# Moving one attention pair's loads ahead of the token weights, and the token weights' conversions behind an earlier pair's state chain

## The chip, the cores and the metric

The kernel runs on one core of one Trainium2 chip. The metric is the device time of one execution in microseconds; the kernel before took 613.91 us (median of three runs, 613.28 to 617.16).

## The reference, cut to what matters

A decayed linear attention in blocks feeds a token-and-channel mixer, and that feeds a Fourier mixer with a channel network.

```python
attn_out = _attn_ref(q, k, v, lam)             # B=2, H=8, S=768, D=64
x = attn_out.transpose(0, 2, 1, 3).reshape(B, S, H * D)
# _moe_ref
xt = x.transpose(0, 2, 1)
h = np.maximum(xt @ w_tok1, 0.0) @ w_tok2      # w_tok1 768x256, w_tok2 256x768
u = x + h.transpose(0, 2, 1)
x = u + np.maximum(u @ w_ch1, 0.0) @ w_ch2     # 512 -> 1536 -> 512
# _moe2_ref: 2-d FFT, norm, 512 -> 2048 -> 512
```

Inside the attention, each block has a scores part (`q k^T` times a decay mask, times `v`) and a state part (`q` times the running `k^T v` state, which decays from block to block).

## The kernel before, in words

The weights arrive as 64-bit words (the host passes double words of the numpy arrays) and are turned into float32 on the chip: ScalarE (ACT) makes `m_*` from the high words (L210), for channel weights also a shifted low word (L213); VectorE (DVE) merges the words (L235, L236, L238 for token weights, L233 and L238 for channel weights). ACT then rounds a high part `w_*` (L264) and GpSimd (POOL) subtracts it from the value for the low part (L265). One call of `convert` moves this chain on by one stage each. Three raw slots of 128x1024 words exist; a load into a slot waits until DVE's last merge has read the slot's old content.

The attention goes by pairs of heads, numbered 0 to 7: 0 to 3 are batch 0, 4 to 7 batch 1. The name of a tile holds the pair's number within its batch. For each pair `s` makes the scores on TensorE (PE) and masks them on DVE (L396), `u` scales `k` on ACT (L413), multiplies it with `v` on PE (L418) and runs the chain of states on DVE (L422 once, L424 four times), and `r` copies the states into a block-diagonal tile `att` on ACT (L435, first two blocks of states, then three), multiplies on PE (L441 with the masked scores, L444 with the states) and copies the result out to `xT` on ACT (L446). `l` loads a later pair: `kp`, then `q`, then `k` and `v` in one. `x` transposes half of a batch's result (PE L461) and splits it (ACT L117, DVE L118), `h` is the first token layer (PE L122 to L124, ACT L498, DVE L499), `o` the second, `m` a step of the channel network.

What stands where in this stretch is written out in the string `EARLY`. PE and SyncE (SP, which issues the loads) follow it literally. ACT, DVE and POOL have an order that a scheduler makes when the kernel is built; `tc.issue_after(ins)` keeps what is issued under it behind `ins`. Each engine runs its own list in order, so one instruction that waits holds all behind it.

The first token layer's three weight tiles are keyed `t1` (`raw_t_0d`, `raw_t_1d`, `raw_t_2d`, 512 KB each), the second's `t2` (`raw_t_0_0d` and so on, 384 KB each). The trace writes `raw_t_0d` for both kinds of the first one.

Of the kernel before, what the change touches and what calls it, by code (L numbers as in the profile page):

```python
# [15 lines left out]
AF = mybir.ActivationFunctionType  # L16
# [10 lines left out]
C = 128  # L27
# [6 lines left out]
BIG = 12 * NQ  # L34


EARLY = """s0 w u0 w s1 r0 u1 s2 u2 l4 r1 s3 c u3 r2 s4 l5 r3 u4 x00 s5 l6 u5 r4 s6 x01 h00 r5 c h01 l7 u6 s7 u7 r6 o00
r7 m o01 x10 m x11 m h10 m h11 m m o10 o11 k"""

WHEN = ((67, 71, 77, 73, 74, 77, 74, 77, 77, 79, 80, 81, 85, 83, 86, 85, 87, 84, 88, 90, 92, 91, 94, 97, 99),  # L40
# [21 lines left out]
def body(ctx: ExitStack, tc: tile.TileContext, qkv, kT, lam, w_tok1, w_tok2,  # L62
# [30 lines left out]


    on_act = {("table", 0): table_load}

    def acc_bank(n):
        return ps_acc.tile([P, 512], F32, tag="acc", name=n)
# [72 lines left out]
    def load_next():  # L171
        job = next_job()
        if job is None:
            return False
        kind, key = job
        at_["load"] += 1
        jobs.append(job)
        raw = raw_p.tile([P, 1024], U32, tag="raw", name="raw_" + "_".join(map(str, key)) + kind[0])
        raws[job] = raw
        if key[0] == "dft":  # L180
            nc.sync.dma_start(raw.bitcast(F32)[:, :512], dft[key[1]])
        elif kind == "sums":
            for i, k in enumerate(pair_keys(key)):
                nc.sync.dma_start(raw.bitcast(F32)[:, i * 512:(i + 1) * 512], singles[place_of(k)])
        elif kind == "single":
            nc.sync.dma_start(raw.bitcast(F32)[:, :512], singles[place_of(key)])
        else:
            w = {"t1": lambda: w_tok1[key[1]], "t2": lambda: w_tok2[key[1], key[2]],
                 "a": lambda: (w_ch1, m_ch1)[key[1]][key[2]], "b": lambda: (w_ch2, m_ch2)[key[1]][key[2]]}[key[0]]()
            nc.sync.dma_start(raw[:, :2 * width(key)], w)  # L190
        return True
# [5 lines left out]
    def stage_abs():  # L197

        if at_["abs"] >= at_["load"]:
            return  # L200
        job = jobs[at_["abs"]]
        kind, key = job
        at_["abs"] += 1
        if kind in ("single", "sums"):
            return
        m = raw_p.tile([P, 512], U32, tag="man", name="m_" + "_".join(map(str, key)), bufs=BUFS["man"])[:, :width(key)]
        mans[job] = m
        with tc.issue_after(on_act["out", 1]):
            lo, hi = words(job)
            nc.scalar.activation(f32(m), f32(hi), AF.Copy, scale=DOWN)  # L210
            if key[0] in "ab":
                halves = raws[job].bitcast(U16)[:, :4 * width(key)].rearrange("p (n t) -> p n t", t=4)
                nc.scalar.activation(lo, halves[:, :, 1], AF.Identity, scale=2.0 ** -13, bias=floor_by)  # L213
# [58 lines left out]
    def convert(n=1, among=()):  # L272

        among = list(among)
        for _ in range(n):
            if at_["part"] < at_["word"] and (jobs[at_["part"]][0] == "ahead" or room(jobs[at_["part"]][1])):
                stage_part()
            if at_["word"] < at_["abs"] and at_["word"] < at_["part"] + 1:
                for op in word_ops():
                    op()  # L280
                    if among:
                        among.pop(0)()
            while at_["load"] < at_["word"] + BUFS["raw"] and len(raws) < BUFS["raw"] and load_next():
                pass
            if at_["abs"] < at_["word"] + 1:
                stage_abs()
        for op in among:
            op()
# [116 lines left out]
    def attention_states(b, hp, dT, pw):  # L405

        n = f"{b}_{hp}"
        t, sts = pair[b, hp]
        kn, v = (t[:, i, :].rearrange("p (c j) -> p c j", j=C) for i in (1, 2))
        behind = (("table", 0), ("state", 0), ("out", 0), ("out", 1))[min(NP * b + hp, 3)]  # L410
        with tc.issue_after(on_act[behind]):
            for a in range(2):
                nc.scalar.activation(kn[:, :NC - 1, a * D:(a + 1) * D], kn[:, :NC - 1, a * D:(a + 1) * D], AF.Copy,  # L413
                                     scale=dT[:, 2 * hp + a, C - 1:C])
        ups = acc_bank(f"u_{n}")
        for c in range(NC - 1):
            for a in range(2):
                nc.tensor.matmul(ups[a * D:(a + 1) * D, c * D:(c + 1) * D], kn[:, c, a * D:(a + 1) * D],  # L418
                                 v[:, c, a * D:(a + 1) * D], start=True, stop=True)
        state = temp((NC - 1) * D, f"state_{n}").rearrange("p (c e) -> p c e", c=NC - 1)  # L420
        up = ups[:, :(NC - 1) * D].rearrange("p (c e) -> p c e", c=NC - 1)
        nc.vector.tensor_copy(state[:, 0], up[:, 0])  # L422
        for c in range(1, NC - 1):
            stt(out=state[:, c], in0=state[:, c - 1], scalar=pw[:, hp, C - 1:C], in1=up[:, c],  # L424
                op0=ALU.mult, op1=ALU.add)
        pair[b, hp] = t, sts, state

    def attention_out(b, hp, bd, bank):
# [560 lines left out]
    with tc.manual_schedule(engines={ENG.SP, ENG.PE}):  # L989
        dT, pw, kps, bds, skew = attention_setup()  # L990

        def load(n):
            load_kp(n // NP, n % NP, kps[n % NP])
            load_qkv(n // NP, n % NP)

        load(2)
        skew(6, H)
        load(3)
        for _ in range(3):
            load_next()  # L1000
        for b in range(B):
            xT[b] = big_tile(f"xT_{b}")[:, :4 * S].rearrange("p (k s) -> p k s", k=4)

        def scores(n):
            attention_scores(n // NP, n % NP, dT, pw, kps[n % NP])

        def states(n):
            attention_states(n // NP, n % NP, dT, pw)

        def result(n):  # L1010
            attention_out(n // NP, n % NP, bds[n % 2], x_bank if n == 7 else acc_bank)


        warm = acc_bank("warm")

        def keep_warm(n):
            for _ in range(n):
                nc.tensor.transpose(warm[:, :P], ident, ident)

        def constants():  # L1020
            rawx = temp(P, "rawx")
            nc.sync.dma_start(rawx, dft_x)
            nc.scalar.activation(cx, rawx, AF.Copy)

        keep_warm(22)
        acts = {"s": scores, "u": states, "r": result, "l": load, "c": convert, "x": token_in, "h": token_hidden,
                "o": token_out, "m": run, "w": lambda: keep_warm(8), "k": constants}
        for word in EARLY.split():
            acts[word[0]](*(int(i) for i in word[1:]))
        run(54 - step["i"])  # L1030
        free = big_tile("tops_0", F32R).rearrange("p (j k h s) -> p j k h s", j=2, k=2, h=2)
        half = half_tile([P, 2, 2, 2, HS], "tops_1", F32R)
        free = [free, big_tile("tops_2", F32R).rearrange("p (j k h s) -> p j k h s", j=2, k=2, h=2)]
        homes = {1: (free[0][:, 0], free[0][:, 1], half[:, 0]), 0: (free[1][:, 0], free[1][:, 1], half[:, 1])}
        pieces = [input_sums(0, k, homes[0]) for k in range(2)]
        for fn in pieces[0]:
            fn()
            run(1)
        run(62 - step["i"])
        for k in range(2):  # L1040
            for fn in input_sums(1, k, homes[1]):
                fn()
        run(64 - step["i"])
        input_sums_last(0, 0)
        for fn in pieces[1]:
            run(1)
            fn()
        run(len(todo) - step["i"])
        for k in range(2):
            input_sums_last(1, k)  # L1050
        pend = [(False, lambda: second(todo[-1]))]

        place = {"i": 0}

        def between():
            j, i = divmod(place["i"], 4)
            place["i"] += 1
            turns = TURNS_7[j] * (i + 1) // 4 - TURNS_7[j] * i // 4
            ends, fn = pend.pop(0) if pend else (False, lambda: None)
            if ends:  # L1060
                fn()
            convert(turns)
            if not ends:
                fn()

        for j, u in enumerate(by_seven):
            seven(u[0], u[1], between)
            last = j == len(by_seven) - 1
            todo_ = seconds(*u)
            if last:  # L1070
                for x in (todo_[0], todo_[2]):
                    second_of(*x)
                second_two(todo_[1], todo_[3])
            else:
                pend.extend([(x[4], lambda x=x: second_of(*x)) for x in todo_])
            if j == 0:
                input_sums_last(0, 1)
# [99 lines left out]
```

## Time and profile before

| what | value |
|---|---|
| median of three runs | 613.91 us (613.28 to 617.16) |
| the profiled execution | 616.56 us, of which the span of the trace is 614.5 us |
| mean granted TensorE clock | 0.997 |
| PE busy | 591.0 us, 96% of the span |
| DVE, ACT, POOL busy | 411.9, 269.8 and 142.6 us |
| moved by DMA | 65.58 MB, mean 107 GB/s |

The profiled execution lies 2.65 us above the median and 2.06 us of it lie outside the span. Times below are in microseconds from the span's start. A row of a timeline gives start, duration, engine, source line, operation, tiles and count, and in brackets how long the engine stood idle before it and what ended that.

### The profile page before, as it was taken

What the parts mean: (1) busy time and instruction counts of PE and PEld (TensorE: products, weight loads), DVE (VectorE), ACT (ScalarE), POOL (GpSimd) and SP (SyncE); (2) the same over time, 40 slices, a digit from 0 to 9 for tenths busy, and PEclk for the clock granted to TensorE, in tenths of its full rate; (3) what the DMA queues carried; (4) which work ended last, traced back from release to release, by engine and by line L of the source; (5) the groups of instructions that cost most, each with busy time, mean ns of one, the idle gap of its engine ahead of it and who ended that gap; (6) DMA issues with size and microseconds to landing.
All of it is one profiled execution on the core that took longest, in us unless ns stands there. A gap on an engine that the chain in (4) does not pass through costs nothing. (4 is left out here: it accounts for less than half of the span.)

```text
span 614.5 us, 9599 instructions
## 1 busy us (share of the span) xinstructions
PE 591.0 (96%) x3704; PEld 546.5 (89%) x3704; DVE 411.9 (67%) x768; ACT 269.8 (44%) x536; POOL 142.6 (23%) x119
## 2 busy tenths in 40 slices
PE   8789999999989999999999999999999999999997
PEld 7767799999989998999989899878888998998896
DVE  6697897792657337649696897789685477343435
ACT  2666984653546345244453462335553454211110
POOL 5254233220400220111263210024420232300000
PEclk9899999999999999999999999999999999999999
DMA  7965434333368247100132101002453132000005
GB/s 278 404 246 190 145 123 158 103 99 126 102 232 272 79 159 259 63 1 1 52 86 70 36 2 34 18 0 71 127 172 112 34 121 86 1 1 0 1 1 205
DMA packets 24637, 65.58 MB, mean 107 GB/s; under 512 B 2824, under 2 KB 3984, under 8 KB 24592
## 3 DMA queue, kind: packets, MB, share of 16 engines
q1 hardware_dynamic: 24304, 64.83, 31.5%
q8 instruction: 29, 0.48, 0.3%
q10 hardware_dynamic: 288, 0.14, 0.1%
q14 instruction: 16, 0.13, 0.1%
HBM read 54.99 MB, written 9.97 MB: 106 GB/s over the span
## 5 line engine op out<-in xcount | busy, mean ns | idle before, releaser
L124 PE MATMUL ac<-w_b,hid 128*128 128x512 f32 x192 | 75.9, 396 | 0.3 <-DVE hid L499 0.3
L123 PE MATMUL ac<-w_b,hid 128*128 128x512 f32 x192 | 75.7, 394 | 0.0
L122 PE MATMUL ac<-w_b,hid 128*128 128x512 f32 x192 | 74.9, 390 | 0.0
L499 DVE SCALAR_TENSOR_TENSOR hid<-ph,hid 128x384 fp32r<-128x384 f32 x68 | 37.7, 554 | 48.8 <-ACT hid L498 48.6
L123 PE MATMUL ac<-hid,w_b 128*128 128x384 f32 x192 | 65.0, 338 | 1.3 <-DVE hid L499 1.1
L122 PE MATMUL ac<-hid,w_b 128*128 128x384 f32 x192 | 65.2, 340 | 1.0 <-ACT hid L498 1.0
L122 PE MATMUL ph<-uh,w_a 128*128 128x384 f32 x192 | 64.7, 337 | 0.5 <-DVE hid L499 0.5
L498 ACT ACTIVATE hid<-ph 128x384 fp32r<-128x384 f32 x68 | 33.0, 485 | 71.7 <-PE ph L124 71.7
L124 PE MATMUL ph<-uh,w_a 128*128 128x384 f32 x192 | 64.3, 335 | 0.0
L124 PE MATMUL ac<-hid,w_b 128*128 128x384 f32 x192 | 64.2, 335 | 0.0
L123 PE MATMUL ph<-uh,w_a 128*128 128x384 f32 x192 | 64.2, 334 | 0.0
L265 POOL TENSOR_TENSOR w_a<-m_a,w_a 128x512 fp32r<-128x512 f32 x18 | 25.6, 1421 | 84.6 <-ACT w_a L264 66.5
L124 PEld LDWEIGHTS ac<-w_b,hid 128*128 128x128 f32 x192 | 36.0, 188 | 8.5 <-DVE hid L499 0.8
L123 PEld LDWEIGHTS ac<-w_b,hid 128*128 128x128 f32 x192 | 36.0, 188 | 6.1
L122 PEld LDWEIGHTS ac<-w_b,hid 128*128 128x128 f32 x192 | 36.1, 188 | 5.8
L265 POOL TENSOR_TENSOR w_b<-m_b,w_b 128x512 fp32r<-128x512 f32 x18 | 24.6, 1368 | 70.2 <-ACT w_b L264 45.6
L122 PEld LDWEIGHTS ac<-hid,w_b 128*128 128x128 f32 x192 | 36.1, 188 | 3.0 <-ACT hid L498 2.5
L123 PEld LDWEIGHTS ac<-hid,w_b 128*128 128x128 f32 x192 | 36.1, 188 | 2.9 <-DVE hid L499 2.9
L122 PEld LDWEIGHTS ph<-uh,w_a 128*128 128x128 f32 x192 | 36.1, 188 | 1.0 <-DVE hid L499 0.8
L123 PEld LDWEIGHTS ph<-uh,w_a 128*128 128x128 f32 x192 | 36.1, 188 | 0.1
L124 PEld LDWEIGHTS ac<-hid,w_b 128*128 128x128 f32 x192 | 36.0, 188 | 0.0
L124 PEld LDWEIGHTS ph<-uh,w_a 128*128 128x128 f32 x192 | 36.0, 188 | 0.0
(504 smaller groups left out, 1478.6 us busy)
## 6 DMA issues: line engine op xcount, KB each, us to landing
qkv<-qkv SPq DMA_DIRECT2D x7, 768.0 KB, 9.4
single_scratch<-m_a SPq DMA_DIRECT2D x16, 256.0 KB, 4.4
qkv<-qkv SPq DMA_DIRECT2D x10, 384.0 KB, 6.0
kp<-kT SPq DMA_DIRECT2D x8, 384.0 KB, 8.4
out<-u SPq DMA_DIRECT2D x11, 256.0 KB, 2.0
single_scratch<-m_b SPq DMA_DIRECT2D x10, 256.0 KB, 5.7
raw_t_0d<-w_tok SPq DMA_DIRECT2D x2, 384.0 KB, 9.1
raw_t_1d<-w_tok SPq DMA_DIRECT2D x2, 384.0 KB, 3.5
```

The costliest lines, as they stand in the source:

```text
L122: nc.tensor.matmul(ps, wt[0], xt[0], start=first, stop=False, **kw)
L123: nc.tensor.matmul(ps, wt[0], xt[1], start=False, stop=False, **kw)
L124: nc.tensor.matmul(ps, wt[1], xt[0], start=False, stop=last, **kw)
L265: nc.gpsimd.tensor_tensor(out=t[:, 1, :n], in0=src, in1=f32(t[:, 0, :n]), op=ALU.subtract)
L498: nc.scalar.activation(hi, ps, AF.Relu)
L499: stt(out=lo, in0=ps, scalar=0.0, in1=f32(hi), op0=ALU.max, op1=ALU.subtract)
```

## The change

`EARLY` is rewritten: the load of pair 4 (`l4`) stands first, then the three loads of the first token layer's weights as `n n n` (they stood ahead of `EARLY` before), the conversion calls `c` that bring those weights forward stand after `u3` and after `l5` and `l6`, and the third pair's result `r2` and the load of pair 6 lie between them. `mark` remembers the latest scaling of `k` on ACT and the latest step of the state chain on DVE, and `behind_urgent` keeps every conversion of a `t1` tile behind what was last marked.

```diff
-EARLY = """s0 w u0 w s1 r0 u1 s2 u2 l4 r1 s3 c u3 r2 s4 l5 r3 u4 x00 s5 l6 u5 r4 s6 x01 h00 r5 c h01 l7 u6 s7 u7 r6 o00
+EARLY = """s0 l4 n n n w u0 w s1 r0 u1 s2 u2 r1 s3 u3 l5 c c r2 l6 c c c s4 r3 u4 x00 s5 u5 r4 s6 x01 h00 r5 c h01 l7 u6 s7 u7 r6 o00
 r7 m o01 x10 m x11 m h10 m h11 m m o10 o11 k"""
+    urgent = {}
+    def mark(which, op):
+        urgent[which] = op.ins
+        return op
+    def behind_urgent(key):
+        stack = ExitStack()
+        if key[0] == "t1":
+            for ins in urgent.values():
+                stack.enter_context(tc.issue_after(ins))
+        return stack
...
-        with tc.issue_after(on_act["out", 1]):
+        with tc.issue_after(on_act["out", 1]), behind_urgent(key):
...
+                key = jobs[at_["word"]][1]
                 for op in word_ops():
-                    op()
+                    with behind_urgent(key):
+                        op()
...
-                nc.scalar.activation(kn[:, :NC - 1, a * D:(a + 1) * D], kn[:, :NC - 1, a * D:(a + 1) * D], AF.Copy,
-                                     scale=dT[:, 2 * hp + a, C - 1:C])
+                mark("act", nc.scalar.activation(
+                    kn[:, :NC - 1, a * D:(a + 1) * D], kn[:, :NC - 1, a * D:(a + 1) * D], AF.Copy,
+                    scale=dT[:, 2 * hp + a, C - 1:C]))
...
-            stt(out=state[:, c], in0=state[:, c - 1], scalar=pw[:, hp, C - 1:C], in1=up[:, c],
-                op0=ALU.mult, op1=ALU.add)
+            mark("dve", stt(out=state[:, c], in0=state[:, c - 1], scalar=pw[:, hp, C - 1:C], in1=up[:, c],
+                            op0=ALU.mult, op1=ALU.add))
...
-        for _ in range(3):
-            load_next()
```

PE's and POOL's lists are the same before and after, row for row. SP's list, from the fourth pair's `k` and `v` on, read before:

```order
L373 DMA qkv_3_170<-qkv 128x1536
L190 DMA raw_t_0d<-w_tok 128x1024
L190 DMA raw_t_1d<-w_tok 128x1024
L190 DMA raw_t_2d<-w_tok 128x1024
L377 DMA kp<-kT 128x768
L372 DMA qkv_0_380<-qkv 128x768
L373 DMA qkv_0_380<-qkv 128x1536
L377 DMA kp<-kT 128x768
L372 DMA qkv_1_513<-qkv 128x768
L373 DMA qkv_1_513<-qkv 128x1536
L377 DMA kp<-kT 128x768
```

and reads now:

```order
L390 DMA qkv_3_170<-qkv 128x1536
L394 DMA kp<-kT 128x768
L389 DMA qkv_0_223<-qkv 128x768
L390 DMA qkv_0_223<-qkv 128x1536
L205 DMA raw_t_0d<-w_tok 128x1024
L205 DMA raw_t_1d<-w_tok 128x1024
L205 DMA raw_t_2d<-w_tok 128x1024
L394 DMA kp<-kT 128x768
L389 DMA qkv_1_457<-qkv 128x768
L390 DMA qkv_1_457<-qkv 128x1536
L205 DMA raw_t_0_0d<-w_tok 128x768
L394 DMA kp<-kT 128x768
```

Pair 4's 1536 KB changed places with the three `t1` tiles' 1536 KB, and the first `t2` tile moved ahead of pair 6.

ACT's list around pair 3 (`qkv_3` and `state_3` are pair 3, `qkv_0` is pair 4, `qkv_1` pair 5, `po_2` and `po_3` the results of pairs 2 and 3) read before:

```order
L210 ACTIVATE m_t_0_437<-raw_t_0d 128x512
L413 ACTIVATE qkv_3_170<-qkv_3_170,att 128x5x64 x2
L210 ACTIVATE m_t_1_716<-raw_t_1d 128x512
L210 ACTIVATE m_t_2_726<-raw_t_2d 128x512
L413 ACTIVATE qkv_0_380<-qkv_0_380,att 128x5x64 x2
L446 ACTIVATE xT_179<-po_2_0_462 128x384
L264 ACTIVATE w_t_0_718<-m_t_0_437 128x512
L435 ACTIVATE att<-state_3_452 64x2x64 x2
L446 ACTIVATE xT_179<-po_2_1_474 128x384
L264 ACTIVATE w_t_1_734<-m_t_1_716 128x512
L435 ACTIVATE att<-state_3_452 64x3x64 x2
L413 ACTIVATE qkv_1_513<-qkv_1_513,att 128x5x64 x2
```

and reads now:

```order
L430 ACTIVATE qkv_3_170<-qkv_3_170,att 128x5x64 x2
L225 ACTIVATE m_t_0_460<-raw_t_0d 128x512
L225 ACTIVATE m_t_1_467<-raw_t_1d 128x512
L430 ACTIVATE qkv_0_223<-qkv_0_223,att 128x5x64 x2
L225 ACTIVATE m_t_2_511<-raw_t_2d 128x512
L453 ACTIVATE att<-state_3_450 64x2x64 x2
L464 ACTIVATE xT_173<-po_2_0_473 128x384
L453 ACTIVATE att<-state_3_450 64x3x64 x2
L464 ACTIVATE xT_173<-po_2_1_485 128x384
L279 ACTIVATE w_t_0_503<-m_t_0_460 128x512
L430 ACTIVATE qkv_1_457<-qkv_1_457,att 128x5x64
L279 ACTIVATE w_t_1_513<-m_t_1_467 128x512
```

Pair 3's scaling now stands ahead of `m_t_0`, and its state copies ahead of the rounding of the token weights, but behind all three `m_t` of the `t1` tiles.

Later on ACT, from the first token layer's second half (`h1s_1_0`) to pair 6's state copies (`state_2`), the list read before:

```order
L498 ACTIVATE h1s_1_0_829<-h_0_1_810 128x512
L413 ACTIVATE qkv_3_834<-qkv_3_834,att 128x5x64
L210 ACTIVATE m_b_0_1029<-raw_b_0d 128x512
L213 ACTIVATE raw_b_0d<-raw_b_0d,floor_by 128x512
L435 ACTIVATE att<-state_2_850 64x2x64 x2
L210 ACTIVATE m_a_1_1039<-raw_a_1d 128x512
L213 ACTIVATE raw_a_1d<-raw_a_1d,floor_by 128x512
L435 ACTIVATE att<-state_2_850 64x3x64 x2
```

and reads now:

```order
L516 ACTIVATE h1s_1_0_829<-h_0_1_810 128x512
L279 ACTIVATE w_a_1_1131<-m_a_1_1039 128x512
L225 ACTIVATE m_a_2_1138<-raw_a_2d 128x512
L228 ACTIVATE raw_a_2d<-raw_a_2d,floor_by 128x512
L453 ACTIVATE att<-state_2_850 64x2x64 x2
L279 ACTIVATE w_b_1_1156<-m_b_1_1064 128x512
L225 ACTIVATE m_b_2_1163<-raw_b_2d 128x512
L228 ACTIVATE raw_b_2d<-raw_b_2d,floor_by 128x512
L279 ACTIVATE w_a_2_1205<-m_a_2_1138 128x512
L453 ACTIVATE att<-state_2_850 64x3x64 x2
```

Four instructions instead of two stand between pair 6's two groups of state copies, and the channel weights converted there are of later tiles; pair 7's scaling (`qkv_3_834`) moved up ahead of these rows.

## Rows read from the trace of the kernel before

**Rows 1.** The page, part 1: busy time, share of the span, instructions.
```profile
PE 591.0 (96%) x3704; PEld 546.5 (89%) x3704; DVE 411.9 (67%) x768; ACT 269.8 (44%) x536; POOL 142.6 (23%) x119
```

**Rows 2.** Table by stage: stretch, length, busy by engine, clock, DMA share, GB/s.
```profile
25.00:60.00 35.00, 30.61 (x393) 26.15 (x390) 28.98 (x61) 24.47 (x54) 14.82 (x11) 1.00 0.64 241
60.00:75.00 15.00, 13.60 (x163) 11.68 (x161) 13.29 (x27) 12.25 (x26) 5.87 (x4) 1.00 0.54 187
75.00:110.00 35.00, 34.42 (x206) 32.01 (x203) 26.98 (x42) 21.89 (x42) 10.72 (x8) 1.00 0.38 123
30.00:35.00 5.00, 3.33 (x55) 2.82 (x50) 5.00 (x12) 2.22 (x6) 2.10 (x2) 1.00 1.04 411
```

**Rows 3.** Waits of PE, 25 to 75 us: total, times, longest.
```profile
PE po L444 <- ACT att L435: 2.8, 4, 1.7
PE u L418 <- ACT qkv L413: 1.4, 2, 0.9
```

**Rows 4.** Timeline of ACT around pair 3 and the first transposes.
```profile
26.39 0.66 ACT L210 ACTIVATE m_t<-raw_t_0d 128x512 f32<-128x512 f32 x1 [0.28 <-DMA raw_t_0d<-w_tok]
26.96 1.00 ACT L413 ACTIVATE qkv<-qkv,att 128x320 f32<-128x320 f32 x2
...
34.57 0.63 ACT L435 ACTIVATE att<-state 64x128 f32<-64x128 f32 x2
...
36.28 0.73 ACT L435 ACTIVATE att<-state 64x192 f32<-64x192 f32 x2
...
39.78 0.63 ACT L264 ACTIVATE w_t<-m_t 128x512 fp32r<-128x512 f32 x1 [1.36 <-DVE m_t L238]
40.32 0.47 ACT L446 ACTIVATE xT<-po 128x384 f32<-128x384 f32 x1
```

**Rows 5.** Timeline of PE, its waits from pair 3 to the token layer.
```profile
27.56 1.19 PE L418 MATMUL u<-qkv 128*64 128x64 f32 x19 [0.87 <-ACT qkv L413]
...
35.01 0.56 PE L444 MATMUL po<-qkv,att 128*64 128x128 f32 x3 [1.68 <-ACT att L435]
36.67 0.71 PE L444 MATMUL po<-qkv,att 128*64 128x128 f32 x3 [0.33 <-ACT att L435]
...
40.85 0.66 PE L461 MATMUL px<-ident,xT 128*128 128x128 f32 x4 [0.87 <-ACT xT L446]
...
52.00 0.50 PE L123 MATMUL h<-x,w_t 128*128 128x512 f32 x1 [0.51 <-DVE x L118]
```

**Rows 6.** Issue of the first token weight, and its time to landing.
```profile
17.01 0.33 SPq L190 DMA_DIRECT2D raw_t_0d<-w_tok  x1
...
raw_t_0d<-w_tok SPq DMA_DIRECT2D x1, 512.0 KB, 9.4
```

**Rows 7.** Timelines of DVE and POOL: the same merge without and with POOL busy.
```profile
27.55 0.69 DVE L236 SCALAR_TENSOR_TENSOR m_t<-raw_t_0d,m_t 128x512 uint32<-128x512 uint32 x1
...
31.46 1.85 DVE L236 SCALAR_TENSOR_TENSOR m_t<-raw_t_1d,m_t 128x512 uint32<-128x512 uint32 x1
...
30.91 1.85 POOL L400 TENSOR_TENSOR qkv<-qkv,att 128x640 f32<-128x640 f32 x1 [6.09 <-DMA qkv<-qkv]
```

**Rows 8.** Timeline of ACT around pair 6's state copies.
```profile
63.00 0.58 ACT L498 ACTIVATE h1s<-h 128x512 fp32r<-128x512 f32 x1
...
65.81 0.71 ACT L210 ACTIVATE m_a<-raw_a_1d 128x512 f32<-128x512 f32 x1
66.42 0.75 ACT L213 ACTIVATE raw_a_1d<-raw_a_1d,floor_by 128x512 uint32<-128x512 uint16 x1
67.07 0.73 ACT L435 ACTIVATE att<-state 64x192 f32<-64x192 f32 x2
```

**Rows 9.** Time to landing of the load behind `m_b_2`.
```profile
raw_b_2d<-w_ch SPq DMA_DIRECT2D x1, 512.0 KB, 3.3
```

**Rows 10.** Timeline of PE: waits at pairs 7 and 6, and later.
```profile
64.08 0.74 PE L418 MATMUL u<-qkv 128*64 128x64 f32 x17 [0.57 <-ACT qkv L413]
...
67.47 0.71 PE L444 MATMUL po<-qkv,att 128*64 128x128 f32 x3 [0.55 <-ACT att L435]
...
90.57 0.45 PE L122 MATMUL ph<-uh,w_a 128*128 128x384 f32 x1 [0.53 <-DVE hid L499]
```

More of the change, by code (lines that the diff above doesn't have):

```diff
@@ L1026, in body @@
         acts = {"s": scores, "u": states, "r": result, "l": load, "c": convert, "x": token_in, "h": token_hidden,
-                "o": token_out, "m": run, "w": lambda: keep_warm(8), "k": constants}
+                "o": token_out, "m": run, "w": lambda: keep_warm(8), "k": constants, "n": load_next}
         for word in EARLY.split():
```

## Prediction

> **What bounds the kernel now.** I read the page's busy shares first, then the table by stage, then the waits of the stage that the change touches. TensorE (PE) is busy 96% of the span [rows 1], so this kernel can only gain where PE stands still, or lose by making it stand still. The table by stage says where that is: from 25 to 60 us, the attention that the change rearranges, PE is busy 30.61 of 35.00 us, so 4.39 us are idle; from 75 to 110 us it is busy 34.42 of 35.00 us [rows 2]. From there on the program is one PE queue whose weights are on time, and a shift of PE at 75 us is a shift of the end. The waits name what PE stands still for in the early stage: ACT's state copies for 2.8 us and ACT's scaling of `k` for 1.4 us [rows 3]. In ACT's timeline the scaling for pair 3 stands directly behind `m_t_0`, which itself waited for its load [rows 4]. PE's order does not change at all, so every term below is the lateness of one operand.
>
> **Which pairs of waits go, and what is late next.** All sums are made against the profiled execution (616.56 us, a span of 614.5 us and 2.06 us outside it) and then carried over to the median of the runs, 613.91 us, as a difference.
>
> Term 1, pair 3's states. ACT stood idle 0.28 us ahead of `m_t_0` at 26.39 us, so it was free at 26.11 us, and the scaling at 26.96 us named no landing of its own [rows 4]. With the scaling first it can start as early as 26.11 us if its load is there, and no later than 26.39 us, since the loads land in order of issue and `m_t_0`'s came behind it. PE waited 0.87 us [rows 5]. I take 0.8 us gained here; the bounds are 0.57 us (26.96 less 26.39) and 0.87 us. In place of `m_t_0` the next limit is PE's own queue.
>
> Term 2, pair 3's result. Pair 4's 1536 KB go ahead of three weights of 512 KB, the same amount. The load rate was 411 GB/s [rows 2], so 1536 KB (1.573 MB) are 3.83 us and 512 KB are 1.28 us. `raw_t_0d` landed 9.4 us after 17.01 us, at 26.4 us [rows 6]; it will land at 30.2 us, and the other two at about 31.5 and 32.8 us. The state chain itself will be done around 30 us, since it no longer shares DVE with merges. But on ACT the copies of pair 3's states stand behind all three `m_t`. The last starts at 32.8 us, and 0.57 us later (26.39 to 26.96 is the pitch of one `m_t`) the copies can start, at about 33.4 to 33.7 us, instead of 34.57 us [rows 4]. So most of this wait stays: PE is at the state product a little earlier and waits for ACT, which now waits for DMA. The first product moves from 35.01 to about 34.1 us; the second group of copies, which stood behind `w_t_1` and the copy of a result (36.28 us), now stands behind that copy alone, so PE's second wait of 0.33 us [rows 5] goes. Pair 3's result ends about 1.1 us earlier in all.
>
> The Trainium skill, DMA: Bandwidth & Descriptors, section "Where 436 GB/s comes from", holds that about 358 GB/s per core bind a load from HBM. This trace moved 411 GB/s in the stretch, so the measurement decides. By the page's figure the swap would be worth 4.4 us of landing instead of 3.8, and the copies would come another 0.6 us later.
>
> Term 3, the first transposes. The last of them waited 0.87 us for the copy of pair 3's second half [rows 5], which stood on ACT behind `w_t_2` at 39.78 us, itself 1.36 us late by DVE's merge [rows 4]. The new list keeps `w_t_2` ahead of this copy. Behind the second state copies, which end at about 35.4 us, ACT has a copy of a result, two roundings, two halves of a scaling, another copy, `m_t_0_0` and `w_t_2` ahead of it: 0.45 + 2 x 0.54 + 1.0 + 0.45 + 0.5 + 0.54 = 4.0 us by the durations and pitches of such rows [rows 4]. The copy starts at about 39.4 to 39.5 us instead of 40.32 us. PE is 0.8 us ahead of the old run at this point; of the 1.1 us, 0.3 are given back. Bounds: 0.4 and 1.1 us.
>
> Term 4, from pair 4's result to the first token layer. DVE now does three merges of the second `t2` tiles ahead of the split that the token layer waited for at 52.00 us [rows 5]: one of the short kind and two of the long, by the row of the 512-wide kind (0.69 us) [rows 7] scaled to 384 columns about 0.5 us each, 1.3 us together with the overlap. They leave the stretch behind, where DVE has room. Against the 0.8 us gained this makes the token layer later by 0.5 us. The lower bound is that DVE has room ahead of it, too (28.98 of 35.00 us busy [rows 2]), and the 0.8 us survive. The upper bound is a merge that meets POOL: the same merge took 0.69 us alone and 1.85 us while POOL scaled `q` [rows 7], so 1.16 us for each one that is caught. I take 0.3 us later, nearer to the row without POOL, with 0.8 us earlier and 1.5 us later as ends.
>
> The Trainium skill, SBUF — State Buffer, section "🔬 SBUF: two separate sides", calls the port pair of VectorE and GpSimd an exclusive lock that the first comer holds for the whole instruction. The rows agree (1.85 us, ending 0.55 us behind POOL's). By that rule every merge that starts under a POOL instruction is caught, and the token layer comes 1.5 us later; with no lock at all it comes 0.5 us later.
>
> Term 5, pairs 7 and 6. Pair 7's scaling moves far up on ACT, so PE's wait of 0.57 us for it [rows 10] goes. But pair 6's second group of state copies now has four instructions ahead of it since the first group (a rounding, `m_b_2` with its low word, another rounding) instead of two. These take, by the pitches 0.61 us (`L210`) and 0.65 us (`L213`) of [rows 8] and 0.54 us for a rounding [rows 4], 2.3 us instead of 1.3 us. PE already waited 0.55 us for the second group [rows 10], so nothing covers the extra 1.0 us. Ahead of the first group three instructions follow `h1s_1_0`, as before. If `h1s_1_0` itself comes when it came (63.00 us [rows 8]; PE's half of it is later by term 4, but the wait of ACT in front of it is shorter), the second product starts 1.0 to 1.2 us later than 67.47 us. I take 1.2 us. Since this wait follows all the others, it swallows terms 1 to 4 whatever they came to: PE only arrives earlier at the same copy.
>
> Term 6, later. Conversions that ran at 80 to 90 us are done earlier. The two ACT instructions ahead of the `hid` that PE waited 0.53 us for at 90.57 us [rows 10] are gone in the new list. I take 0.5 us back, between 0 and 0.53.
>
> The sum is 1.2 - 0.5 = 0.7 us later: 617.3 us against the profiled 616.56 us, and **614.6 us** on the scale of the median. With the ends of terms 5 and 6 the forecast's own range is 613.5 to 615.8 us.
>
> **Rivals.** First, faster. The copies of pair 6 are not the last word if everything that feeds them (loads into raw slots, merges, `h1s_1_0`) moves forward with the early gain. For it: in the old run ACT was busy 24.47 and DVE 28.98 of 35.00 us [rows 2], and the first channel weights' loads now get their slots several us earlier. Then the 0.8 us of term 3, the 0.57 us of pair 7 and the 0.5 us of term 6 add up to 1.9 us: 612.0 us. Against it: the order puts more conversions ahead of the copies, not fewer.
>
> Second, slower by one mechanism at pair 6. `m_b_2` stands between the two groups of state copies, so ACT cannot make the second group before `raw_b_2d` has landed, 3.3 us after its issue [rows 9], and the issue waits until DVE has merged `m_a_1` out of the slot. From that last merge on there follow 3.3 us of load, 0.61 + 0.65 us for `m_b_2`, 0.54 us for a rounding and 0.4 us to PE, 5.5 us in all. It decides from the point where this merge ends later than 63.2 us (68.7 less 5.5, the forecast's start of the second product). If DVE is 2.3 us later than that, because merges meet POOL (two at 1.16 us), PE starts at 71.0 us, 3.5 us later than before: 613.91 + 3.5 - 0.5 = 616.9 us. For it: the 1.85 us row. Against it: the load chain starts earlier than before.
>
> Third, the change does nothing where it aims: ACT and DVE hold conversions back until the weights land anyhow, 3.8 us later, and the places where PE stands still are only renamed. That is 613.9 us. SP belongs here, too: the load of `t2`'s first tile waits on SP for DVE's merge of `m_t_0` (about 34.6 us), with pair 6's loads behind it; but by the load rate above these land about 1 us later than before, at about 41.5 us, and pair 6's scores stand in PE's queue behind pair 4's result, several us after the transposes of 40.85 us [rows 5]; that cover hides it.
>
> **How the numbers follow.** The forecast (614.6 us) gets 0.44, the faster rival 0.23, the slower one 0.27, no effect 0.06. A measurement of this kernel cannot tell less than about 1% (6.1 us) from no change, and the idle time in the touched stretch is itself under 6 us (4.39 us from 25 to 60 us and 1.40 us to 75 us [rows 2]). So faster by over 1% gets 0.02, slower by over 1% 0.04 (a second copy of the slow mechanism at pair 7 or at a weight that comes late), within 1% 0.94. The range goes from the faster rival to somewhat past the slower one, since the runs before alone span 613.28 to 617.16 us: 611.8 to 617.4 us.
>
> **What the profile after would show.** Right: pair 3's scaling within 0.3 us of 26.1 us and no wait of PE at its state product of about 26.8 us; `m_t_0` on ACT at about 30.2 us behind an idle time that its load ends; pair 3's state copies at 33.4 to 33.8 us; PE still waiting for them for over 1 us; the copy ahead of the last transpose at about 39.5 us; no wait at pair 7's scaling; a wait of 1.5 us or more at pair 6's second state product, with `m_b_2` in front of it on ACT. Wrong: that product earlier than 67.5 us (the faster rival), or ACT idle for `raw_b_2d` right between the two groups of copies (the slower one). A wait of PE for token or channel weights, or for pair 6's loads, would show a mechanism that I priced at nothing.

## The result, and the profile after

The changed kernel took 623.3 us (median of six runs, 620.42 to 624.8) beside 615.44 us for the kernel before (six runs, 613.28 to 617.16): a ratio of 1.0121, with a 95% interval of 1.0096 to 1.0146. It is slower by 1.2%, 5.9 us past the top of the range. The profiled execution after took 624.8 us, with a span of 622.7 us, 8.2 us more than before.

The page's row of TensorE and the table by stage answer to [rows 1, 2]. The columns after the length of a stretch are the busy times of PE, PE's weight loads, DVE, ACT and POOL, the granted TensorE clock, the DMA share and GB/s.

```profile
PE 592.6 (95%) x3704; PEld 548.7 (88%) x3704; DVE 412.3 (66%) x768; ACT 270.6 (43%) x536; POOL 141.4 (23%) x119
...
25.00:60.00 35.00, 27.64 (x354) 23.91 (x355) 29.75 (x61) 23.44 (x51) 14.89 (x10) 0.95 0.73 267
60.00:75.00 15.00, 8.78 (x105) 7.03 (x104) 11.74 (x17) 11.92 (x23) 7.50 (x8) 0.90 0.49 174
75.00:110.00 35.00, 35.00 (x234) 33.34 (x235) 24.48 (x47) 20.68 (x42) 6.18 (x5) 0.95 0.31 108
...
35.00:38.00 3.00, 2.83 (x27) 2.87 (x29) 3.00 (x4) 2.67 (x7) 1.65 (x2) 0.52 0.72 232
...
72.00:78.00 6.00, 3.97 (x29) 3.15 (x26) 5.71 (x13) 4.59 (x10) 2.55 (x2) 0.50 0.52 175
```

PE's busy time over the whole program grew by 1.6 us (592.6 against 591.0 us), so 6.6 of the 8.2 us are idle time. From 25 to 60 us PE is idle for 7.36 us (4.39 before), from 60 to 75 us for 6.22 us (1.40 before), and from 75 to 110 us it is busy without a gap. At 78 us PE is 8.5 us behind (below), at the end 8.2 us: the loss is made before that, as the prediction's reading of the stages had it. The two short stretches show where the added busy time comes from: at 35 and at 72 us PE ran at half its clock, 1.2 instead of 2.4 GHz.

PE's waits answer to [rows 5, 10]; each row gives the start of the work behind the wait, and the wait in brackets.

```profile
25.56 1.19 PE L436 MATMUL u<-qkv 128*64 128x64 f32 x19 [0.57 <-ACT qkv L430]
...
35.17 0.71 PE L462 MATMUL po<-qkv,att 128*64 128x128 f32 x3 [3.83 <-ACT att L453]
...
45.65 0.80 PE L436 MATMUL u<-qkv 128*64 128x64 f32 x20 [2.08 <-DVE x L133]
...
63.17 0.39 PE L139 MATMUL h<-x,w_t 128*128 128x512 f32 x1
...
71.20 0.56 PE L462 MATMUL po<-qkv,att 128*64 128x128 f32 x3 [4.20 <-ACT att L453]
...
74.91 0.86 PE L462 MATMUL po<-qkv,att 128*64 128x128 f32 x3 [2.03 <-ACT att L453]
...
77.62 0.69 PE L137 MATMUL ht<-w_t,h1s 128*128 128x384 f32 x1
```

The kernel before, at the same places of PE, of ACT (pair 6's first copies) and of DVE (the first and the last step of pair 6's states):

```profile
60.59 0.39 PE L124 MATMUL h<-x,w_t 128*128 128x512 f32 x1
...
65.59 0.56 PE L444 MATMUL po<-qkv,att 128*64 128x128 f32 x3 [0.28 <-ACT att L435]
...
69.09 0.45 PE L122 MATMUL ht<-w_t,h1s 128*128 128x384 f32 x1
...
65.16 0.62 ACT L435 ACTIVATE att<-state 64x128 f32<-64x128 f32 x2
...
64.22 0.21 DVE L422 COPY state<-u 128x64 f32<-128x64 f32 x1
...
66.37 0.28 DVE L424 SCALAR_TENSOR_TENSOR state<-state,att,u 128x64 f32<-128x64 f32 x1
```

The large new waits are the two at pair 6 (71.20 and 74.91 us, 6.23 us together, 0.83 before). PE is 2.6 us late when it ends the token layer's second half (`h`, 63.17 us instead of 60.59). At pair 6 the first state product starts 5.6 us later than before, the second 7.4 us later, and the second token product behind them (`ht`, 77.62 us instead of 69.09) 8.5 us later. ACT's timeline around pair 6, which answers to [rows 8], shows what stands ahead of the copies (L453):

```profile
64.13 0.68 ACT L225 ACTIVATE m_a<-raw_a_1d 128x512 f32<-128x512 f32 x1 [0.91 <-DMA raw_a_1d<-w_ch]
...
65.89 0.70 ACT L225 ACTIVATE m_b<-raw_b_1d 128x512 f32<-128x512 f32 x1
...
67.13 0.61 ACT L516 ACTIVATE h1s<-h 128x512 fp32r<-128x512 f32 x1
...
68.71 0.67 ACT L225 ACTIVATE m_a<-raw_a_2d 128x512 f32<-128x512 f32 x1
...
70.74 0.64 ACT L453 ACTIVATE att<-state 64x128 f32<-64x128 f32 x2 [0.71 <-DVE state L442]
...
71.95 0.66 ACT L225 ACTIVATE m_b<-raw_b_2d 128x512 f32<-128x512 f32 x1
...
73.97 0.63 ACT L279 ACTIVATE w_a<-m_a 128x512 fp32r<-128x512 f32 x1 [0.73 <-DVE m_a L253]
74.51 0.73 ACT L453 ACTIVATE att<-state 64x192 f32<-64x192 f32 x2
```

The token layer's `h1s_1_0` (L516) starts at 67.13 us instead of 63.00. Ahead of it stand the conversions of `m_a_1`, which waits 0.91 us for its load, and of `m_b_1`. Between it and the first copies stand those of `m_a_2`, and between the copies those of `m_b_2`. DVE shows the same, since each conversion has merges there (L248, L253) and POOL's subtraction of `w_*` (L280) beside them:

```profile
68.48 0.68 DVE L517 SCALAR_TENSOR_TENSOR h1s<-h,h1s 128x512 fp32r<-128x512 f32 x1
69.08 0.21 DVE L440 COPY state<-u 128x64 f32<-128x64 f32 x1
69.21 1.31 DVE L253 SCALAR_TENSOR_TENSOR m_b<-raw_b_1d,m_b 128x512 uint32<-128x512 uint32 x1
70.44 0.27 DVE L442 SCALAR_TENSOR_TENSOR state<-state,att,u 128x64 f32<-128x64 f32 x1
...
72.22 1.72 DVE L253 SCALAR_TENSOR_TENSOR m_a<-raw_a_2d,m_a 128x512 uint32<-128x512 uint32 x1
73.87 0.27 DVE L442 SCALAR_TENSOR_TENSOR state<-state,att,u 128x64 f32<-128x64 f32 x1
...
76.05 0.68 DVE L253 SCALAR_TENSOR_TENSOR m_b<-raw_b_2d,m_b 128x512 uint32<-128x512 uint32 x1
...
68.69 1.28 POOL L280 TENSOR_TENSOR w_a<-m_a,w_a 128x512 fp32r<-128x512 f32 x1 [1.29 <-ACT w_a L279]
72.12 1.28 POOL L280 TENSOR_TENSOR w_b<-m_b,w_b 128x512 fp32r<-128x512 f32 x1 [2.15 <-DVE m_a L248]
```

Two merges stand inside pair 6's chain of five state steps, and both overlap a subtraction on POOL: they take 1.31 and 1.72 us; the same line took 0.68 us at 76.05 us, between two subtractions, and [rows 7] show the like. The chain takes from 69.08 to 74.14 us, 5.06 us, where it took 2.43 us before (64.22 to 66.65 us). Of the two engines it is mostly DVE that ends last: DVE's half of `h1s_1_0` (L517, 68.48 us) follows the merges of `m_a_1` and `m_b_1` without a gap and the chain of states follows it, the first copies on ACT wait 0.71 us for the state step behind the merge of 1.31 us, and ahead of the second copies the rounding of `m_a_2` (73.97 us) waits 0.73 us for the merge of 1.72 us.

Around pair 3, ACT's timeline answers to [rows 4]:

```profile
24.95 1.01 ACT L430 ACTIVATE qkv<-qkv,att 128x320 f32<-128x320 f32 x2 [0.77 <-DMA qkv<-qkv]
30.76 0.67 ACT L225 ACTIVATE m_t<-raw_t_0d 128x512 f32<-128x512 f32 x1 [4.80 <-DMA raw_t_0d<-w_tok]
32.03 0.66 ACT L225 ACTIVATE m_t<-raw_t_1d 128x512 f32<-128x512 f32 x1 [0.60 <-DMA raw_t_1d<-w_tok]
32.60 1.00 ACT L430 ACTIVATE qkv<-qkv,att 128x320 f32<-128x320 f32 x2
34.15 0.68 ACT L225 ACTIVATE m_t<-raw_t_2d 128x512 f32<-128x512 f32 x1 [0.56 <-DMA raw_t_2d<-w_tok]
34.73 0.62 ACT L453 ACTIVATE att<-state 64x128 f32<-64x128 f32 x2
...
40.85 0.47 ACT L464 ACTIVATE xT<-po 128x384 f32<-128x384 f32 x1
```

Pair 3's copies are about as late as before (34.73 against 34.57 us), behind three conversions that wait for loads. PE was there earlier and stood longer, 3.83 us.

### The profile page after: what moved, and what is told of

It reads as the page before. It is cut to its first block, busy times and chain, and to the rows that moved or that the text cites. A ratio compares the mean times of both kernels' runs of the same rounds, so it can differ in the third digit from the quotient of the medians.

```text
span 622.7 us, 9597 instructions
## 1 busy us (share of the span) xinstructions
PE 592.6 (95%) x3704; PEld 548.7 (88%) x3704; DVE 412.3 (66%) x768; ACT 270.6 (43%) x536; POOL 141.4 (23%) x119
## 5 line engine op out<-in xcount | busy, mean ns | idle before, releaser
L517 DVE SCALAR_TENSOR_TENSOR hid<-ph,hid 128x384 fp32r<-128x384 f32 x68 | 37.6, 553 | 50.1 <-ACT hid L516 49.8
L516 ACT ACTIVATE hid<-ph 128x384 fp32r<-128x384 f32 x68 | 33.0, 486 | 72.8 <-PE ph L139 72.7
L280 POOL TENSOR_TENSOR w_b<-m_b,w_b 128x512 fp32r<-128x512 f32 x18 | 24.5, 1364 | 81.8 <-ACT w_b L279 55.1
L280 POOL TENSOR_TENSOR w_a<-m_a,w_a 128x512 fp32r<-128x512 f32 x18 | 24.3, 1352 | 81.9 <-ACT w_a L279 63.7
```

The source lines that it names most:

```text
L280: nc.gpsimd.tensor_tensor(out=t[:, 1, :n], in0=src, in1=f32(t[:, 0, :n]), op=ALU.subtract)
L516: nc.scalar.activation(hi, ps, AF.Relu)
L517: stt(out=lo, in0=ps, scalar=0.0, in1=f32(hi), op0=ALU.max, op1=ALU.subtract)
```

## The experiments

**Theory A**: the loss is made at pair 6. The moved conversion calls let the scheduler bring the channel weights' conversions forward, on ACT and DVE, ahead of `h1s_1_0` and of pair 6's states; the long waits also cost TensorE's clock. **Rival B**: the load order makes it, since the token weights now land 3.8 us later and ACT is held at pair 3. **Rival C**: the holding by `issue_after` makes it. The five calls `c` ahead of `r3` do what one call, and `h00` four times more, did before: `h00` converts until its weights are there, so by its end both programs have issued the same conversions. Those of the channel weights come behind `r6` in both, and it is the scheduler that puts them ahead of `h1s_1_0`. In the edits below only the changed words of `EARLY` are quoted; "before" numbers are medians on the same chip.

**Loads alone (e1).** The file of after with pair 4's loads ahead of the token weights, the conversion calls and the loads of pairs 5 and 6 in their old places and no holding.

```diff
-s0 l4 n n n w ... r1 s3 u3 l5 c c r2 l6 c c c s4 r3 u4 x00 s5 u5
+s0 l4 n n n w ... r1 s3 c u3 r2 s4 l5 r3 u4 x00 s5 l6 u5
-        if key[0] == "t1":
+        if False:
```

> Only the order of the loads is changed (pair 4's loads ahead of the three token weights); the conversion calls stand where they stood before and nothing holds them back. ACT's list is the one of before but for one pair of neighbours. Theory A (the loss of about 8 us is made at pair 6, by channel weights' conversions that ACT and DVE run ahead of pair 6's state copies, and comes with the moved conversion calls): no loss at pair 6, PE's waits there stay near 0.3 and 0.6 us, time within 2 us of before (613 to 617 us). Rival B (the token weights land 3.8 us later and push every later conversion and load back): 3 to 8 us slower than before, with the wait at pair 6 grown to several us.

Measured: 617.55 us beside 615.25, ratio 1.004 (1.0024 to 1.0057). Its waits of PE:

```profile
32.48 1.68 PE L436 MATMUL u<-qkv 128*64 128x64 f32 x19 [7.38 <-ACT qkv L430]
...
69.17 0.56 PE L462 MATMUL po<-qkv,att 128*64 128x128 f32 x3 [0.30 <-ACT att L453]
...
71.04 0.71 PE L462 MATMUL po<-qkv,att 128*64 128x128 f32 x3 [0.54 <-ACT att L453]
```

Pair 6 waits as it did before. What is lost is lost elsewhere: without the holding, `m_t_0` stands ahead of pair 3's scaling on ACT and now waits for a later load, and PE stands 7.38 us at pair 3's states. That is in the profiled execution (620.09 us), whose span is 3.6 us longer than that of before; the median is 2.3 us longer, just over the 2 us that theory A allowed. Waits that came later fall away. So this load order does not make the loss of after.

**Conversions alone (e2).** Pair 4's loads behind the token weights again, the calls moved and held as in after (the second token layer's loads go with the calls).

```diff
-s0 l4 n n n w u0 w s1 r0 u1 s2 u2 r1 s3 u3
+s0 n n n w u0 w s1 r0 u1 s2 u2 l4 r1 s3 u3
```

> Only the conversions are moved and held behind the fourth pair's chain; the loads of the token weights stay ahead of pair 4's. ACT's list from the token layer to pair 6 is the one of the changed kernel. Theory A: the loss stays, 5 to 8 us slower than before, with PE waiting 4 us or more at pair 6's first state product. Rival B: most of the loss goes, within 2 us of before, since the weights land as early as before.

Measured: 621.69 us beside 615.25, ratio 1.0109 (1.0076 to 1.0142). PE's waits:

```profile
34.18 0.56 PE L462 MATMUL po<-qkv,att 128*64 128x128 f32 x3 [0.70 <-ACT att L453]
...
70.67 0.56 PE L462 MATMUL po<-qkv,att 128*64 128x128 f32 x3 [3.71 <-ACT att L453]
74.39 0.86 PE L462 MATMUL po<-qkv,att 128*64 128x128 f32 x3 [2.39 <-ACT att L453]
```

With the old load order and only 0.70 us of wait at pair 3, pair 6 waits 6.10 us (3.71 us of it at the first product, where theory A said 4 or more), and this kernel loses 6.4 us where after loses 7.9. B falls as the main cause.

**Part of the channel conversions held back (e4).** After, with the channel weights from the third pair of tiles on (`m_a_2`, `m_b_2`) held behind pair 6's state copies.

```diff
+        if key[0] in "ab" and key[1] == 0 and key[2] >= 2 and ("state", 6) in on_act:
+            stack.enter_context(tc.issue_after(on_act["state", 6]))
         return stack
```

> The changed kernel with the conversions of the channel weights from the third pair of tiles on (m_a_2, m_b_2 and later) held behind pair 6's state copies. Theory A: PE's wait of 2.03 us at pair 6's second state product goes, and the half-speed clock behind it is shorter; the first wait (4.2 us) stays nearly whole, since the second pair of tiles still stands ahead of it; 2 to 4 us faster than the changed kernel, about 619 to 621 us. Rival B: no gain, 622 to 624 us.

Measured: 619.78 us beside 615.25, ratio 1.0073 (1.0052 to 1.0093). The second wait at pair 6 is gone, the first (3.20 us at 70.05) stays, for `m_a_1` and `m_b_1` still stand ahead of `h1s_1_0`.

**One weight pair more held back (e5)**: `key[2] >= 1` in the same line.

> The same with the second pair of tiles (m_a_1, m_b_1) held back, too. Theory A: h1s_1_0 comes on ACT within 1.5 us of the end of its matmuls, both waits at pair 6 fall under 1 us together, TensorE's clock stays at full speed there, and the time is back at that of before or under it: 613 to 617 us. If the loss were only passed on to a channel weight that now comes late, PE would wait for w_a or w_b after 78 us and the time stay at 619 us or more. Rival B: no gain.

Measured: 617.46 us beside 615.25, ratio 1.004 (1.002 to 1.006).

```profile
34.11 0.72 PE L464 MATMUL po<-qkv,att 128*64 128x128 f32 x3 [3.30 <-ACT att L455]
...
45.43 0.80 PE L438 MATMUL u<-qkv 128*64 128x64 f32 x20 [1.80 <-DVE x L135]
...
71.03 0.45 PE L139 MATMUL ht<-w_t,h1s 128*128 128x384 f32 x1
```

No wait is left at pair 6, the granted clock is 1.00 from 60 to 75 us (0.90 in after), and of the 7.9 us over the kernel before 2.2 are left, just over what theory A allowed (617 us). A holds for 5.7 of the 7.9 us, by doing the one thing it names. The weights held back are not missed: from 75 to 110 us PE is busy 34.59 of 35.00 us. The waits at pair 3 and pair 5 are nearly as in after, and what is left of the loss is made there: PE ends the token layer's second half 3.5 us later than before (its last matmul starts at 64.12 us, 60.59 before), and starts `ht` 1.9 us later (71.03 against 69.09 us).

**The holding taken out (e3).** After's `EARLY`, with `if False:` in place of `if key[0] == "t1":`.

> The changed kernel with the same string, but nothing holds the token weights' conversions behind the fourth pair's chain. Its list on ACT from the token layer to pair 6 keeps nearly the order of the changed kernel. Theory A (the moved conversion calls bring the channel weights' conversions ahead of pair 6's state copies): the loss stays, 621 to 625 us. Rival C (the holding back itself delays the conversions and with them everything later): back to within 3 us of before, 613 to 618 us.

Measured: 623.63 us beside 615.44, ratio 1.0126 (1.0092 to 1.016), as slow as after, with 3.06 us of wait at pair 3 and 3.38 us at pair 6 (in the profiled execution, 621.63 us). The holding makes no part of the loss that can be told; C falls.

**The token conversions behind pair 3's copies (e6).** After's loads, the calls `c` behind `r3`, and the `t1` conversions also held behind pair 3's state copies.

```diff
-u3 l5 c c r2 l6 c c c s4 r3 u4
+u3 l5 r2 l6 s4 r3 c c c c c u4
+            stack.enter_context(tc.issue_after(on_act["state", 3]))
```

> Pair 4's loads first as in the changed kernel, the conversion calls only behind pair 3's result, and the token weights' conversions behind pair 3's state copies on ACT, too, so that ACT does not wait for a load ahead of these copies. Expected: PE's wait of 3.8 us at pair 3's first state product goes (under 0.5 us) and the clock stays at full speed there; but ACT's list around pair 6 still has channel weights' conversions ahead of the state copies. Theory A with a share of its own for each place: 2 to 4 us faster than the changed kernel, 619 to 622 us. If pair 6's chain alone sets the time from 70 us on, whatever came before, the time stays at 622 to 624 us.

Measured: 620.65 us beside 615.44, ratio 1.0076 (1.0049 to 1.0103). The wait at pair 3 is gone, one of 2.16 us stands at the first transposes, and pair 6 still waits 1.57 and 3.21 us. It is 2.7 us faster than after, as theory A with a share for each place had it.

**Both mended (e7)**: the last kernel with the holding of channel weights (`key[2] >= 1`) as well.

> The same, with the channel weights' conversions from the second pair of tiles on held behind pair 6's state copies. Theory A: both places mended, 2 to 3 us faster than the version with pair 6 mended alone (617.5 us), about 613.5 to 616 us, so at the time of before or just under it. If the wait at pair 3 only turns into a wait for loads of pair 5, no gain over 617 us.

Measured: 616.51 us beside 615.44, ratio 1.0014 (0.9994 to 1.0033).

```profile
38.01 2.18 PE L482 MATMUL px<-ident,xT 128*128 128x128 f32 x9 [4.28 <-ACT xT L467]
...
66.48 0.65 PE L465 MATMUL po<-qkv,att 128*64 128x128 f32 x3 [0.78 <-ACT att L456]
```

The loss is gone within what can be told, with the new load order kept. Of the 7.9 us, 6.8 came back, where the two mendings alone gave 5.7 and 2.7, so the two places overlap. The 613.5 to 616 us of theory A are missed by 0.5 us: nothing is won, since the early wait now stands at the transposes.

**The holding put into the kernel before (e8).** This asks whether the held channel weights gain anything by themselves.

```diff
-        with tc.issue_after(on_act["out", 1]):
+        with ExitStack() as stack:
+            stack.enter_context(tc.issue_after(on_act["out", 1]))
+            if key[0] in "ab" and key[1] == 0 and key[2] >= 1 and ("state", 6) in on_act:
+                stack.enter_context(tc.issue_after(on_act["state", 6]))
```

> The kernel before, with nothing changed but that channel weights' conversions from the second pair of tiles on are held behind pair 6's state copies. It tells whether holding back costs something later: PE's waits of 0.28 and 0.55 us at pair 6 go, and unless a channel weight comes late behind 75 us the time is 0 to 1 us under before, 614 to 615.5 us. If the hold has a price of its own, slower by 1 to 3 us, and the versions with the hold carry that price.

Measured: 616.41 us beside 615.44, ratio 1.0011 (0.999 to 1.0032): no difference, and so not the 0 to 1 us under before that was expected, nor a price of the holding. Of pair 6's waits 0.29 us stay, and pair 7's states wait 1.02 and 0.60 us for their scaling.

**A gain sought, twice.** First (e9), in the kernel with both mended, pair 5's scaling held behind pair 3's last result copy:

```diff
+        if NP * b + hp == 5:
+            behind = ("out", 3)
         with tc.issue_after(on_act[behind]):
```

> The kernel of e7 with one line more: pair 5's scaling on ACT may not come before pair 3's last result copy. In e7 that scaling stood ahead of the two xT copies and waited 3.05 us for GpSimd, and TensorE waited 4.28 us at 38.01 us for the copies. Theory A (the loss of the change sits only in what stands ahead of the copies that TensorE needs on ACT, at the pairs 3 and 6): the wait at the transposes falls under 1 us, they end near 36.5 us instead of 40.1, pair 5's scores follow, and of the 3.6 us gained at 40 us some 2 to 3.5 are left at the end, 613 to 614.5 us, a ratio of 0.995 to 0.999 to the kernel before. Rival B (pair 6 gives everything back: its copies wait for the same conversions of the channel weights whatever the time of arrival): the wait at the first state product of pair 6 grows from 0.78 us to 3 or more, and the time stays at 616 to 617 us. Rival C (pair 5's load is the next thing that is late): the scores of pair 5 wait 2 us or more behind the transposes, and the time stays at 616 us.

Measured: 617.04 us beside 615.88, ratio 1.0023 (1.0004 to 1.0041).

```profile
35.48 0.77 PE L484 MATMUL px<-ident,xT 128*128 128x128 f32 x5 [0.26 <-ACT xT L469]
39.14 0.66 PE L484 MATMUL px<-ident,xT 128*128 128x128 f32 x4 [2.89 <-ACT xT L469]
42.98 0.33 PE L441 MATMUL u<-qkv 128*64 128x64 f32 x2 [1.65 <-DVE x L136]
44.84 1.22 PE L441 MATMUL u<-qkv 128*64 128x64 f32 x17 [1.53 <-ACT qkv L435]
```

The transposes start 2.5 us earlier, as theory A had it, but one of 2.89 us follows among them: the second copy now stands behind a rounding of `w_t_0` that waits 2.65 us for a merge on DVE, and pair 5's states then wait for DVE's split and for the scaling itself. The expected gain fails, and by a cause that none of the three forecasts named: neither pair 6 (0.69 us) nor pair 5's load.

Second (e10), in the kernel before with the holding, pair 4's scaling held behind pair 3's state copies:

```diff
+        if NP * b + hp == 4:
+            behind = ("state", 3)
         with tc.issue_after(on_act[behind]):
```

> The kernel of e8 (the kernel before with the channel conversions held behind pair 6's copies) with pair 4's scaling held behind pair 3's state copies on ACT: the same kind of order that the change gives pair 3 by other means, by one line and without moving a load or a conversion. In e8 the scaling waited 3.04 us for its load up to 33.28 us, pair 3's first state copies followed at 35.09 us although the fourth state step on DVE had ended at 33.70, and TensorE waited 1.85 us at 35.53. Theory A: the wait falls to 0.5 us or less, and 1 to 1.4 us are gained at 36 us; as the pairs behind it hardly wait in e8 (0.60 and 1.02 us at pair 6's states), half of it is left at the end: 615.3 to 616 us, within what can be told from the 616.4 us of e8. Rival B (the scaling of pair 4 is then what is late): TensorE waits 1 us or more for ACT ahead of pair 4's states at 38 us, and the time is 616.4 to 617.5 us.

Measured: 615.82 us beside 615.88, ratio 1.0008 (0.999 to 1.0025).

```profile
33.96 0.63 ACT L267 ACTIVATE w_t<-m_t 128x512 fp32r<-128x512 f32 x1 [2.49 <-DVE m_t L241]
...
34.90 0.71 PE L449 MATMUL po<-qkv,att 128*64 128x128 f32 x3 [1.77 <-ACT att L440]
```

The wait of 1.85 us only changes its cause (1.77 us are left): a rounding of the token weights now stands ahead of the second copies and waits 2.49 us for DVE. The time lies in the range that theory A gave, but by luck, since the gain it named did not come. No kernel here beats the one before.

## Why the prediction was wrong

**The step that failed is term 5**, its size and one assumption in it. It said that the wait at pair 6 swallows what the earlier terms gain, and that is what happened. But it took 1.2 us, and the second product came 7.4 us later (74.91 against 67.47 us). Of these, 4.1 us stand ahead of `h1s_1_0` on ACT (67.13 against 63.00 us), 1.5 us between it and the first copies (3.61 against 2.16 us) and 1.9 us between the two groups of copies (3.77 against 1.91 us); the term had nothing, nothing and 1.0 us for the three. The assumption "If `h1s_1_0` itself comes when it came (63.00 us ...)" was wrong by 4.1 us. The reason given, that ACT's wait ahead of it would be shorter, looked at the wait and not at the list: `m_a_1` (with a load that was late) and `m_b_1` now stand ahead of it. The new list in "The change" says so, if indirectly: the rounding of `m_a_1` stands directly behind `h1s_1_0`. PE's last matmul for it started at 63.17 us, 2.6 us later than before, so PE accounts for part of the 4.1 us at most, and ACT and DVE were the late ones. Over the kernel before, holding the later weights back brought the 7.9 us down to 4.5, and holding these back as well to 2.2. Second, the term counted ACT's instructions and none of DVE's. The two groups were 3.8 us apart, not the 2.9 us (1.9 before and 1.0 more) that the term makes of them, because the rounding ahead of the second one waited 0.73 us for a merge that POOL made long, and the last state step stood behind the same merge. The Trainium skill, SBUF — State Buffer, section "🔬 SBUF: two separate sides", says that the lock holds for the whole instruction; the 1.31 and 1.72 us rows agree with it, each ending 0.54 or 0.55 us behind POOL's subtraction, and the prediction weighed it at term 4 but not here.

**A term was missing**: the clock. Behind the waits of 3.83 and 4.20 us the granted clock was 0.52 and 0.50 of full (1.2 GHz). Pair 6's second half took 2.71 us from 74.91 to 77.62 us, before 1.62 us from 67.47 to 69.09 us: 1.1 us on top of the waits, and the start of `ht` runs slow, too (the clock is 0.79 from 78 to 80 us). That this adds up: from 25 to 110 us PE is idle 7.2 us more than before, from 15 to 25 us 0.8 us less, 6.4 us of the 8.2 us of span; slower work of this kind is what the other 1.8 us leave room for (PE's busy time over the whole program grew by 1.6 us). The clock was not changed by itself in any run, so this share is worked out and not shown apart.

**The slow rival** had the place right and half of the mechanism: merges did meet POOL. The other half did not come, since ACT shows no idle time for `raw_b_2d` between the copies. The late things were the lists ahead of `h1s_1_0` and the merges, so the 616.9 us that the rival gave was too small as well.

**Terms 1 to 3**, pair 3 and the transposes. Pair 3's scaling came at 24.95 us, not 26.1, with its own load as the releaser, so 0.57 us of wait stayed where none was expected. Most of the lead came from the front: pair 1's states ran at 15.85 us instead of 17.69, which varies between executions (last section). The three `m_t` were 0.5 to 1.4 us later than forecast (30.76, 32.03 and 34.15 us against 30.2, 31.5 and 32.8), and the copies came at 34.73 instead of 33.4 to 33.7 us. Pair 4's scaling of 1.00 us stands among them, as the list in "The change" has it, and the sum left it out; but `m_t_2` still waited 0.56 us for its load behind it, so the third load set the time. As forecast PE still waited over 1 us there, and the second wait of 0.33 us went. The copy ahead of the last transpose came at 40.85 us, 1.4 us behind the forecast. The wait at pair 7's scaling went, as forecast.

**Term 4** had the mechanism of its upper bound in another place. The wait at the token layer (52.00 us) is gone. DVE's split, held up by merges (one of 1.75 us at 43.05 us), now stops PE earlier, 2.08 us at pair 5's states. **Term 6** was right: the wait of 90.57 us is gone, but it followed a loss that it could not touch.

**The chances** went wrong with term 5. Slower by over 1% got 0.04 on the ground that the idle time in the stretch was under 6 us. That bounds what can be gained; it says nothing of what a new wait can cost. The forecast's own range, 613.5 to 615.8 us, does not follow from the ends it names, either: 1.0 to 1.2 us of term 5 less 0 to 0.53 of term 6 are 614.4 to 615.1 us. Of the signs, the wait of 1.5 us or more at pair 6's second product came (2.03 us); none spoke of the 4.20 us at the first.

## What to carry to other kernels

In a list that an engine runs in order, work out the lateness of an operand from everything that now stands ahead of its producer, on each engine of its chain, and not only from what was put between producer and consumer. Work for later that is brought forward by a change of the order is best held behind the copies that the busiest engine needs next: one such line (`issue_after` on pair 6's copies) gave back 5.7 of 7.9 us here. And where the engines around the bound one are busy for two thirds to 85% of a stretch, as ACT and DVE are here, a wait that is taken away tends to come back one instruction further on: wherever the wait between 31 and 46 us stood, the kernels that kept pair 6 free came out within 0.4% of the kernel before.

## What the runs showed of the hardware

A wait of PE of about 4 us was followed by half the clock for 3 us of work at 35 us and for over 6 us at 72 us; the 2.08 us at 45.65 us was not (1.00 from 45 to 50 us). The length of the wait alone does not tell: the 1.80 us at 45.43 us in the kernel with `m_a_1` and `m_b_1` held back, too, was followed by half the clock (0.50 from 47 to 49 us), and so was one of 1.79 us at 44.33 us in the kernel with part of them held (0.50 from 46 to 48 us). In the kernel with the loads alone a wait of 7.38 us went with a span longer by 3.6 us. And the front of the program varies between profiles of kernels with one load order: pair 1's states ran at 15.85 us in after and in the kernel before with the holding, whose loads are in the old order, but at 17.69 us in the kernel before and in the one with `t1` behind pair 3's copies, whose loads are in the new one. The granted clock from 15 to 25 us was 1.00 in the first two and 0.83 in the others. The kernel before and the one with the holding have the same lists there, up to 25 us; what differs is the load of `att` that ACT's scaling for pair 1 waits for: issued at 9.1 to 9.2 us, it landed after 7.9 us in the one and after 6.0 us in the other. Each kernel has one profile here, so this does not show how often it happens. A gain of 1.8 us read there from two profiles would not have been the change's.
